# Attention and feed-forward on one core: float32 scores in two row halves, and a shorter rounding of the first batch's weights

## The chip, the cores and the metric

The kernel runs on one core of a Trainium2 chip. The metric is the time of one execution on the device in microseconds; the figure for a kernel is the median of several runs. The profile is of one execution. The engines are TensorE (PE, its weight loads PEld), VectorE (DVE), ScalarE (ACT), GpSimd (POOL) and SyncE (SP), which here only issues transfers.

## The reference

Causal attention for 4 batches of 12 heads (448 positions, 64 numbers a head), then a feed-forward layer with a layer norm ahead and a residual. Inputs are float32, but the two weight matrices reach the kernel as float64 words.

```python
scores = (1 / sqrt(64)) * matmul(q, k.T)          # per batch and head: 448 x 448
scores = where(triu(ones, k=1), -1e9, scores)
attn = exp(scores - max(scores))
attn = attn / (sum(attn) + 1e-09)
a = matmul(attn, v)                               # heads side by side: x is 448 x 768
xn = (x - mean(x)) / sqrt(var(x) + 1e-06) * g_ln
out = x + maximum(xn @ w_ch1, 0) @ w_ch2          # 768 -> 3072 -> 768
```

## The kernel before, in words

Heads go in pairs (6 pairs a batch), and a head's 448 rows in four blocks of 112. Row block `i` needs only the first 112 x (i + 1) columns of the scores, so a head has 112 + 224 + 336 + 448 = 1120 columns.

**Feed-forward.** Every product is made of three float32r products of high and low parts: `wh` with `xh`, `wh` with `xl`, `wl` with `xh` (L416), and likewise for the second layer (L435). `ffn` is a generator that yields after every 18 products of 448 columns; such a piece is a *slot*. A batch has 48 slots. The accumulators `ph` and `po` have two buffers. After a `ph`, ScalarE writes `hh` (Relu, L421) and VectorE `hl` (L422).

**Weights.** 48 units of 128 x 768 words, one per slot. In the first batch a unit is loaded as float64 words (`raw`, five buffers), rounded to float32, kept in DRAM for the later batches (`keep`), and split into `wh` (ScalarE, L116) and `wl` (L121). Rounding is `convert1` (GpSimd L93 and ScalarE L96, both from the high words) and `convert2` (two passes of VectorE, L101 and L105). `wl` is made by GpSimd in the first batch, by VectorE in the others. `weights_ahead` puts these steps into the slots: a unit used in slot s is begun in slot s - 4, with `convert2`, `split1` and `split2` one, two and three slots later. The first four units are rounded while batch 0's attention runs.

**Attention.** `scores` gives TensorE the products of a group of row blocks; VectorE reduces each block with the mask and finds its minimum (L237), `exps` is ScalarE's, `norm` multiplies by the reciprocal of the sum (GpSimd in batch 0, VectorE later; L267), `transposes` turns the probabilities (L283) and `pv` multiplies by v (`px`, L298), float32, with the two heads in the two column halves of the array. Scores of batch 0 are one float32 product over all 128 rows (L222), with the other head's rows of q filled with zeros by GpSimd (L166, L167). Scores of the later batches are two float32r products (L229): `split1` and `split2` make `qs` (q rounded in the upper 64 rows, its remainder in the lower) and `kh`, `kl`, on ScalarE (L187), VectorE (L188, L195) and GpSimd (L198).

**What sets the order.** All engines' queues are in the order in which the code is written. The lists at the top say in which slot, counted from the pair's own, each group of scores (`SAT`), of transposes (`TAT`), each head's norm (`NAT`) and the pair's `pv` (`END`) stand; the names with a 0 are batch 0's, which has no slots of products around it. In a slot the loop writes the steps of `pre` (loads, exponentials, norm), then the weights' steps, then 18 products, then the steps of `post` (`pv`, transposes, scores). The attention of batch b + 1 is woven into batch b's feed-forward slots.

Of the kernel before, what the change touches and what calls it, by code (L numbers as in the profile page):

```python
# [19 lines left out]
P = 128  # L20
C = 112
# [8 lines left out]
SGROUPS = [[(0, 3)], [(0, 0), (0, 2)], [(0, 1), (1, 1)], [(1, 3)], [(1, 0), (1, 2)]]  # L30
# [8 lines left out]
TH0, TH = [38, 40], [18, 30]  # L39
ELAG = [2, 5, 7]  # L40
NDVE = 7
STATS = [(0, 3), (3, 5), (5, 6)]
OFF = [C * (i * (i + 1) // 2) for i in range(NC + 1)]
# [3 lines left out]
def kernel(ctx, tc, qk, v, w1, w2, g, out):  # L47
# [26 lines left out]
    raw, zs, w32, wh, wl = {}, {}, {}, {}, {}  # L74
# [77 lines left out]
    class Att:  # L152
# [10 lines left out]
        def load(self, p):  # L163
            if self.b == 0:
                r = (first_qk if p < 4 else more_qk)[:, p % 4 * 3:p % 4 * 3 + 3, :]
                nc.gpsimd.memset(r[D:, 0, :], 0.0)  # L166
                nc.gpsimd.memset(r[:D, 1, :], 0.0)  # L167
                nc.sync.dma_start(out=r[:D, 0:3:2, :], in_=qk[0, p][:D, 0:3:2, :])
                nc.sync.dma_start(out=r[D:, 1:3, :], in_=qk[0, p][D:, 1:4:2, :])
            else:  # L170
                r = sb.tile([P, 4, S], F32, tag="qkraw", name="qkraw", bufs=1)
                nc.sync.dma_start(out=r, in_=qk[self.b, p])
            if self.b == 0:
                vt = rest[:C, 2 * NC * D * p:2 * NC * D * (p + 1)]
# [4 lines left out]
            self.t["raw", p], self.t["v", p] = r, vt  # L179

        def split1(self, p):
            r = self.t["raw", p]
            qs = sb.tile([P, 2, S], F32R, tag="qs", name="qs", bufs=1)
            kh = sb.tile([P, 2, S], F32R, tag="kh", name="kh", bufs=1)
            kl = sb.tile([P, 2, S], F32R, tag="kl", name="kl", bufs=1)
            rq, rk = r[:, 0:2, :], r[:, 2:4, :]
            nc.scalar.activation(out=qs, in_=rq, func=ACTF.Copy)  # L187
            nc.vector.tensor_copy(kh, rk)  # L188
            self.t["qk", p] = qs, kh, kl

        def split2(self, p):
            r = self.t.pop(("raw", p))
            qs, kh, kl = self.t["qk", p]
            rq, rk = r[:, 0:2, :], r[:, 2:4, :]
            nc.vector.tensor_tensor(  # L195
                out=qs[D:], in0=rq[D:], in1=qs[D:].bitcast(F32), op=ALU.subtract
            )
            nc.gpsimd.tensor_tensor(out=kl, in0=rk, in1=kh.bitcast(F32), op=ALU.subtract)  # L198

        def scores(self, p, grp):  # L200
            if self.b == 0:
                tag, bufs = (("sc", 3), ("sc", 3), ("sc", 3), ("mm", 2), ("mm", 2))[self.turn % 5]
                self.turn += 1
            else:
                tag, bufs = "sc", 3
# [155 lines left out]
        def steps(self):  # L361
# [4 lines left out]
            def put(where, t, f, *a):  # L366
                where.setdefault(t, []).append((f, a))
# [168 lines left out]
```

## Time and profile before

| | before |
|---|---|
| median of 3 runs | 960.81 us (958.25 to 961.01) |
| span of the profiled execution | 955.6 us |
| median less that span | 5.2 us |
| TensorE, busy | 908.6 us, 95% |
| VectorE, busy | 626.7 us, 66% |
| ScalarE, busy | 416.8 us, 44% |
| GpSimd, busy | 283.1 us, 30% |
| chain that ended last, TensorE's share | 65% |
| memory traffic over the span | 150 GB/s |

The span runs from the first to the last instruction of the one profiled execution; that execution has no time of its own beside it, so the median of the runs stands for it. Busy shares are means over stages that differ, so they don't say what bounds a stage. TensorE's products are pipelined: a product's duration in a row is longer than the distance from its start to that of the next.

### The profile page before, as it was taken

The page shows a single profiled execution, that of the slowest core. Times are in us where ns is not written, and L with a number is a line of the kernel's source. Part 1 is how long each engine was busy: PE and PEld are TensorE (multiplying, and loading weights), DVE is VectorE, ACT ScalarE, POOL GpSimd, SP SyncE. Part 2 cuts the span into 40 slices and gives each one's busy share as a digit, 9 for nine tenths or more (in the row PEclk, how much of TensorE's full clock was granted, in tenths as well). Part 3 has the DMA queues.
Part 4 walks back from the last instruction along what each step waited for, and adds up shares of the span by engine and source line. Part 5 has one row for each costly group of instructions (what it writes and reads, how often), then busy time and mean ns, then how long its engine had stood idle before and what let it go on. Part 6 is the DMA issues. An engine that isn't in the chain of part 4 may idle for free.

```text
span 955.6 us, 13000 instructions
## 1 busy us (share of the span) xinstructions
PE 908.6 (95%) x4864; PEld 794.1 (83%) x4864; DVE 626.7 (66%) x1208; ACT 416.8 (44%) x859; POOL 283.1 (30%) x211
## 2 busy tenths in 40 slices
PE   6888988998998799999999999999999999999998
PEld 4556877887787698898888998898888999999997
DVE  5978999999989746656565566666665544333432
ACT  6754565547553344444543245443443233323320
POOL 7654675887758901111010311110010210000000
PEclk9988998999999999999999999999999999999999
DMA  9730667767677654332322463323322243233310
GB/s 252 270 112 1 213 232 270 250 221 278 217 249 239 234 192 147 115 135 80 134 80 76 150 226 115 139 87 137 115 100 76 98 165 116 100 103 119 108 56 36
DMA packets 35246, 144.36 MB, mean 151 GB/s; under 512 B 4080, under 2 KB 8688, under 8 KB 35184
## 3 DMA queue, kind: packets, MB, share of 16 engines
q1 hardware_dynamic: 35184, 143.54, 43.5%
q8 instruction: 38, 0.62, 0.3%
q14 instruction: 24, 0.20, 0.1%
HBM read 119.15 MB, written 24.38 MB: 150 GB/s over the span
## 4 chain that ended last, share of the span: by engine, by line
PE 65%; POOL 0%; DVE 0%; ACT 0%; issue 0%; POOLq 0%; ACTq 0%
PE po L435 29%; PE ph L416 28%; PE sc L229 3%; PE px L298 3%; PE pt L283 2%; PE pln L311 1%; POOL wl L121 0%; PE rb L336 0%; PE mb L331 0%; DVE w L105 0%; ACT wh L116 0%; DVE xT L439 0%; POOL xl L356 0%; POOLq L121 0%; ACTq L116 0%
## 5 line engine op out<-in xcount | busy, mean ns | idle before, releaser
L435 PE MATMUL po<-hh,wl 128*128 128x448 f32 x576 | 212.7, 369 | 8.7 <-POOL wl L121 8.7
L416 PE MATMUL ph<-xh,wh 128*128 128x448 f32 x576 | 215.2, 374 | 3.4 <-DVE hl L422 2.0
L435 PE MATMUL po<-hh,wh 128*128 128x448 f32 x576 | 215.6, 374 | 0.0
L416 PE MATMUL ph<-xl,wh 128*128 128x448 f32 x576 | 212.1, 368 | 0.5 <-POOL xl L356 0.5
L416 PE MATMUL ph<-xh,wl 128*128 128x448 f32 x576 | 211.4, 367 | 1.0 <-POOL wl L121 1.0
L435 PE MATMUL po<-hl,wh 128*128 128x448 f32 x576 | 212.0, 368 | 0.0
L422 DVE SCALAR_TENSOR_TENSOR hl<-ph,hh 128x448 fp32r<-128x448 f32 x96 | 59.7, 622 | 128.1 <-ACT hh L421 128.1
L116 ACT ACTIVATE wh<-full 128x768 fp32r<-128x768 f32 x144 | 119.5, 839 | 54.8 <-PE po L435 50.8
L121 DVE TENSOR_TENSOR wl<-full,wh 128x768 fp32r<-128x768 f32 x144 | 136.3, 953 | 0.8 <-ACT wh L116 0.5
L198 POOL TENSOR_TENSOR kl<-qkraw,kh 128x896 fp32r<-128x896 f32 x18 | 48.2, 2678 | 278.8 <-DVE kh L188 267.3
L251 ACT ACTIVATE P<-P,nm 112x448 f32<-112x448 f32 (+3 forms) x176 | 91.7, 522 | 81.9 <-DVE nm L237 77.9
L435 PEld LDWEIGHTS po<-hh,wl 128*128 128x128 f32 x576 | 109.2, 190 | 20.4 <-POOL wl L121 11.6
L421 ACT ACTIVATE hh<-ph 128x448 fp32r<-128x448 f32 x96 | 51.9, 540 | 162.8 <-PE ph L416 162.7
L416 PEld LDWEIGHTS ph<-xh,wh 128*128 128x128 f32 x576 | 109.2, 190 | 13.0 <-DVE hl L422 2.3
L416 PEld LDWEIGHTS ph<-xh,wl 128*128 128x128 f32 x576 | 108.9, 189 | 10.3 <-POOL wl L121 1.7
L435 PEld LDWEIGHTS po<-hh,wh 128*128 128x128 f32 x576 | 109.4, 190 | 8.5
L416 PEld LDWEIGHTS ph<-xl,wh 128*128 128x128 f32 x576 | 109.1, 189 | 8.8 <-POOL xl L356 0.9
L435 PEld LDWEIGHTS po<-hl,wh 128*128 128x128 f32 x576 | 109.3, 190 | 8.2
L121 POOL TENSOR_TENSOR wl<-w,wh 128x768 fp32r<-128x768 f32 x48 | 103.2, 2151 | 36.8 <-issue 15.2
L439 DVE TENSOR_TENSOR xT<-po,xT 128x448 f32<-128x448 f32 x48 | 29.9, 622 | 115.6 <-PE po L435 115.6
L237 DVE CUSTOM_DVE_ANT_0 P<-sc,mask 112x448 f32<-112x448 f32 (+3 forms) x176 | 70.2, 443 | 38.2 <-PE sc L229 26.6
L105 DVE SCALAR_TENSOR_TENSOR w<-w,z 128x768 uint32<-128x768 uint32 x48 | 90.0, 1875 | 3.1
(64 smaller groups left out, 1049.0 us busy)
## 6 DMA issues: line engine op xcount, KB each, us to landing
full<-scratch SPq DMA_DIRECT2D x72, 768.0 KB, 4.2
raw<-w_dram SPq DMA_DIRECT2D x48, 768.0 KB, 4.9
scratch<-w SPq DMA_DIRECT2D x48, 384.0 KB, 2.7
qkraw<-qk_dram SPq DMA_DIRECT2D x18, 896.0 KB, 7.2
out_dram<-xT SPq DMA_DIRECT2D x24, 224.0 KB, 2.0
vt<-v_dram SPq DMA_DIRECT2D x18, 224.0 KB, 5.6
first_qk<-qk_dram SPq DMA_DIRECT2D x8, 224.0 KB, 5.3
rest<-v_dram SPq DMA_DIRECT2D x6, 224.0 KB, 7.4
```

The costliest lines, as they stand in the source:

```text
L105: nc.vector.scalar_tensor_tensor(out=w, in0=w, scalar=3, in1=z, op0=ALU.logical_shift_left, op1=ALU.bitwise_or)
L116: nc.scalar.activation(out=wh[s], in_=w32[s], func=ACTF.Copy)
L121: eng.tensor_tensor(out=wl[s], in0=w32[s], in1=wh[s].bitcast(F32), op=ALU.subtract)
L198: nc.gpsimd.tensor_tensor(out=kl, in0=rk, in1=kh.bitcast(F32), op=ALU.subtract)
L229: nc.tensor.matmul(pt[:, o:o + n], lhsT=qs[:, h, C * i:C * i + C], rhs=kk[:, h, :n], start=(part == 0), stop=(part == 1),)
L237: nc.vector.tensor_tensor_reduce(out=self.t["P", p, h][:, OFF[i]:OFF[i + 1]], in0=pt[:, o:o + n], in1=mask[:, S - n:], op0=ALU.add, op1=AL ...
L251: nc.scalar.activation(out=pp, in_=pp, func=ACTF.Exp, scale=-1.0, bias=nm[:, x:x + 1], accum_out=self.t["sm", p, h][:, i:i + 1],)
L416: nc.tensor.matmul(pm[y], lhsT=w[:, c * P:c * P + P], rhs=z[:, c, :], start=(c == 0 and i == 0), stop=(c == KC - 1 and i == 2),)
L421: nc.scalar.activation(out=hh[:, x + y, :], in_=pm[y], func=ACTF.Relu)
L422: nc.vector.scalar_tensor_tensor(out=hl[:, x + y, :], in0=pm[y], scalar=0.0, in1=hh[:, x + y, :].bitcast(F32), op0=ALU.max, op1=ALU.subtract,)
L435: nc.tensor.matmul(pm, lhsT=w[:, o:o + P], rhs=z[:, x, :], start=(x == 0 and i == 0), stop=(x == HF - 1 and i == 2),)
L439: nc.vector.tensor_tensor(out=a.xT[:, m, :], in0=pm, in1=a.xT[:, m, :], op=ALU.add)
```

## The change

Rounding: `convert1` is two passes of ScalarE, a Prelu with two slopes on the high words and a copy from integers, with a scale, on the low words. `convert2` is one pass of VectorE. GpSimd has no part in it, and `wl` is always VectorE's. Scores: q and k are loaded once per head, one head into the upper 64 rows and one into the lower, and each row block of each head is one float32 product over 64 rows, for all batches. Nothing is split or filled with zeros. A group is now a list of row blocks for both heads, each head with an accumulator of its own, and three slots hold a pair's scores. Norm, transposes and `pv` of a later pair stand one slot later, and the probabilities have four buffers instead of three.

```diff
-SGROUPS = [[(0, 3)], [(0, 0), (0, 2)], [(0, 1), (1, 1)], [(1, 3)], [(1, 0), (1, 2)]]
+SGROUPS = [[3], [0, 2], [1]]
...
-SAT0, TAT0, NAT0, END0, EV0 = [-1, 0, 2, 2, 4], [7, 8, 9, 10, 11], [4, 6], 13, [1, 1, 0, 1, 0]
-SAT, TAT, NAT, END, EV = [0, 0, 1, 1, 2], [3, 4, 4, 5, 5], [3, 4], 6, [1, 1, 0, 0, 0]
+SAT0, TAT0, NAT0, END0, EV0 = [-1, 1, 3], [7, 8, 9, 10, 11], [5, 6], 13, [1, 1, 0, 1, 0]
+SAT, TAT, NAT, END, EV = [0, 1, 2], [4, 5, 5, 6, 6], [4, 5], 7, [1, 1, 0, 0, 0]
...
     def convert1(s):
-        high = raw[s][:, :, 1].bitcast(F32)
-        zs[s] = sb.tile([P, UH], F32, tag="z", name="z", bufs=3)
+        bits[s] = sb.tile([P, UH], U32, tag="bits", name="bits", bufs=3)
         w32[s] = sb.tile([P, UH], F32, tag="w32", name="w32", bufs=4)
-        nc.gpsimd.tensor_scalar(
-            out=zs[s], in0=high, scalar1=0.0, scalar2=1.0, op0=ALU.mult, op1=ALU.mult
+        nc.scalar.activation(
+            out=w32[s], in_=raw[s][:, :, 1].bitcast(F32), func=ACTF.Prelu, scale=2.0 ** -112,
+            alpha=2.0 ** 32,
         )
-        nc.scalar.activation(out=w32[s], in_=high, func=ACTF.Copy, scale=2.0 ** -112)
+        nc.scalar.activation(
+            out=bits[s], in_=raw.pop(s)[:, :, 0], func=ACTF.Copy, scale=LAST * 2.0 ** -29
+        )
 
     def convert2(s):
         ready.add(s)
-        z, w = zs.pop(s).bitcast(U32), w32[s].bitcast(U32)
+        w = w32[s].bitcast(U32)
         nc.vector.scalar_tensor_tensor(
-            out=z, in0=raw.pop(s)[:, :, 0], scalar=29, in1=z,
-            op0=ALU.logical_shift_right, op1=ALU.bitwise_or,
-        )
-        nc.vector.scalar_tensor_tensor(
-            out=w, in0=w, scalar=3, in1=z, op0=ALU.logical_shift_left, op1=ALU.bitwise_or
+            out=w, in0=w, scalar=3, in1=bits.pop(s), op0=ALU.logical_shift_left,
+            op1=ALU.bitwise_or,
         )
...
     def split2(s):
         wl[s] = sb.tile([P, UH], F32R, tag="wl", name="wl", bufs=4)
-        eng = nc.gpsimd if s < ns else nc.vector
-        eng.tensor_tensor(
+        nc.vector.tensor_tensor(
             out=wl[s], in0=w32[s], in1=wh[s].bitcast(F32), op=ALU.subtract
         )
...
-                r = (first_qk if p < 4 else more_qk)[:, p % 4 * 3:p % 4 * 3 + 3, :]
-                nc.gpsimd.memset(r[D:, 0, :], 0.0)
-                nc.gpsimd.memset(r[:D, 1, :], 0.0)
-                nc.sync.dma_start(out=r[:D, 0:3:2, :], in_=qk[0, p][:D, 0:3:2, :])
-                nc.sync.dma_start(out=r[D:, 1:3, :], in_=qk[0, p][D:, 1:4:2, :])
-            else:
-                r = sb.tile([P, 4, S], F32, tag="qkraw", name="qkraw", bufs=1)
-                nc.sync.dma_start(out=r, in_=qk[self.b, p])
-            if self.b == 0:
+                r = first_qk[:, 2 * p:2 * p + 2, :]
                 vt = rest[:C, 2 * NC * D * p:2 * NC * D * (p + 1)]
                 vt = vt.rearrange("p (h j d) -> p h j d", h=2, j=NC)
             else:
+                r = sb.tile([P, 2, S], F32, tag="qkraw", name="qkraw", bufs=2)
                 vt = sb.tile([C, 2, NC, D], F32, tag="v", name="vt", bufs=2)
+            nc.sync.dma_start(out=r[:D], in_=qk[self.b, p][:D, 0:3:2, :])
+            nc.sync.dma_start(out=r[D:], in_=qk[self.b, p][D:, 1:4:2, :])
             nc.sync.dma_start(out=vt, in_=v[self.b, p])
...
-                if self.b == 0:
-                    r = self.t["raw", p]
+            r = self.t["qk", p]
+            o = 0
+            for i in grp:
+                n = C * (i + 1)
+                for h in range(2):
                     nc.tensor.matmul(
-                        pt[:, o:o + n], lhsT=r[:, h, C * i:C * i + C], rhs=r[:, 2, :n],
-                        start=True, stop=True,
+                        tiles[h][:, o:o + n], lhsT=r[D * h:D * h + D, 0, C * i:C * i + C],
+                        rhs=r[D * h:D * h + D, 1, :n], start=True, stop=True,
                     )
-                else:
-                    qs, kh, kl = self.t["qk", p]
-                    for kk, part in ((kh, 0), (kl, 1)):
-                        nc.tensor.matmul(
-                            pt[:, o:o + n], lhsT=qs[:, h, C * i:C * i + C], rhs=kk[:, h, :n],
-                            start=(part == 0), stop=(part == 1),
-                        )
                 o += n
...
                 if self.b:
                     put(pre, t0 - 4, self.load, p)
-                    put(pre, t0 - 2, self.split1, p)
-                    put(pre, t0 - 1, self.split2, p)
```

Where the instructions then stand. TensorE first, at a later pair's `pv` in the full stretches. `sc` are the scores, `px` the product with v, and each row is a product with its result's rows and columns. Before:

```order
L298 MATMUL px<-PT,vt 64x448 x2
L298 MATMUL px<-PT,vt 64x336 x2
L298 MATMUL px<-PT,vt 64x224 x2
L298 MATMUL px<-PT,vt 64x112 x2
L229 MATMUL sc<-kh,qs 112x448
L229 MATMUL sc<-kl,qs 112x448
L229 MATMUL sc<-kh,qs 112x112
L229 MATMUL sc<-kl,qs 112x112
L229 MATMUL sc<-kh,qs 112x336
L229 MATMUL sc<-kl,qs 112x336
```

And of the change, at the same place:

```order
L278 MATMUL px<-PT,vt 64x448 x2
L278 MATMUL px<-PT,vt 64x336 x2
L278 MATMUL px<-PT,vt 64x224 x2
L278 MATMUL px<-PT,vt 64x112 x2
L206 MATMUL sc<-qkraw 112x112 x2
L206 MATMUL sc<-qkraw 112x336 x2
```

Behind `px` stood one head's blocks 3, 0 and 2; now blocks 0 and 2 of both heads stand there, block 3 of both a slot before and block 1 of both a slot later.

VectorE, in batch 0's attention, where the second early unit is rounded (`z` and `w` are L101 and L105; `r` is the reciprocal that releases GpSimd's norm; `ISA P,nm<-sc` is the reduction of a score block). Before:

```order
L262 TENSOR_SCALAR r<-sm 112x4
L263 RECIPROCAL r<-r 112x4
L237 ISA rest,nm<-sc,mask 112x112
L237 ISA nm 112x1
L237 ISA rest,nm<-sc,mask 112x336
L237 ISA nm 112x1
L101 SCALAR_TENSOR_TENSOR z<-raw,z 128x768
L105 SCALAR_TENSOR_TENSOR w_283<-w_283,z 128x768
L237 ISA rest,nm<-sc,mask 112x224
```

And of the change:

```order
L242 TENSOR_SCALAR r<-sm 112x4
L243 RECIPROCAL r<-r 112x4
L126 TENSOR_TENSOR wl<-w_182,wh 128x768
L110 SCALAR_TENSOR_TENSOR w_274<-w_274,bits 128x768
L216 ISA rest,nm<-sc,mask 112x112
L216 ISA nm 112x1
L216 ISA rest,nm<-sc,mask 112x336
```

The two passes of one unit have become the `wl` of the unit before and one pass, and the reductions that stood between the reciprocal and the first pass now stand behind both.

ScalarE, in one slot of the first layers with exponentials in it (`hh` is the Relu). Before:

```order
L251 ACTIVATE P,sm<-P,nm 112x448
L251 ACTIVATE P,sm<-P,nm 112x112
L251 ACTIVATE P,sm<-P,nm 112x336
L96 ACTIVATE w_1186<-raw 128x768
L116 ACTIVATE wh<-w_1074 128x768
L421 ACTIVATE hh<-ph 128x448
```

And of the change:

```order
L231 ACTIVATE P,sm<-P,nm 112x112
L231 ACTIVATE P,sm<-P,nm 112x336
L231 ACTIVATE P,sm<-P,nm 112x112
L231 ACTIVATE P,sm<-P,nm 112x336
L99 ACTIVATE w_1207<-raw 128x768
L103 ACTIVATE bits<-raw 128x768
L122 ACTIVATE wh<-w_1080 128x768
L399 ACTIVATE hh<-ph 128x448
```

One more pass of 128 x 768 stands ahead of the Relu, and the exponentials of a slot are those of both heads.

## Rows read from the trace of the kernel before

**Rows 1.** Busy time by stage: stretch, its length, each engine, granted clock, DMA share, GB/s.
```profile
0.00:84.00 84.00, 66.29 (x368) 42.09 (x368) 62.24 (x178) 48.82 (x143) 45.29 (x79) 0.93 0.58 180
84.00:100.00 16.00, 13.21 (x54) 11.31 (x55) 15.60 (x28) 9.56 (x18) 9.90 (x10) 0.85 0.17 53
100.00:340.00 240.00, 217.14 (x1150) 187.77 (x1150) 218.60 (x300) 125.50 (x235) 180.17 (x98) 0.97 0.69 239
340.00:558.00 218.00, 218.00 (x1216) 195.25 (x1215) 133.63 (x311) 92.75 (x198) 25.29 (x13) 1.00 0.36 125
558.00:776.00 218.00, 218.00 (x1216) 195.26 (x1215) 132.82 (x310) 91.93 (x197) 22.48 (x12) 1.00 0.34 120
```

**Rows 2.** TensorE's waits, 84 to 340 us: total us, times, longest.
```profile
PE pt L283 <- DVE P L267: 13.1, 11, 2.5
PE po L435 <- POOL wl L121: 8.7, 7, 1.9
PE ph L416 <- DVE hl L422: 2.0, 1, 2.0
PE ph L416 <- ACT xh L353: 1.4, 1, 1.4
PE ph L416 <- POOL wl L121: 1.0, 2, 0.5
```

**Rows 3.** Chain of waits, one pair of batch 2: start, us, what.
```profile
565.44 0.92 PE sc L229 x6
...
570.02 0.81 PE sc L229 x6
...
574.49 0.51 PE sc L229 x4
...
591.60 2.04 PE px L298 x16
593.64 1.10 PE sc L229 x6
```

**Rows 4.** Timeline of TensorE in batch 0, scores and then px: start, us.
```profile
20.40 1.68 PE L222 MATMUL sc<-first_qk 128*112 128x448 f32 x6
22.01 2.11 PE L298 MATMUL px<-PT,rest 112*64 112x448 f32 x16
```

**Rows 5.** Groups of VectorE, 84 to 340 us: busy us, mean ns; idle before.
```profile
L105 DVE SCALAR_TENSOR_TENSOR w<-w,z 128x768 uint32<-128x768 uint32 x44 | 86.1, 1957 | 2.7
L101 DVE SCALAR_TENSOR_TENSOR z<-raw,z 128x768 uint32<-128x768 uint32 x44 | 54.1, 1230 | 0.2
...
L195 DVE TENSOR_TENSOR qs<-qkraw,qs 64x896 fp32r<-64x896 f32 x5 | 11.5, 2292 | 0.2
...
L121 DVE TENSOR_TENSOR wl<-full,wh 128x768 fp32r<-128x768 f32 x1 | 0.9, 950 | 0.0
```

**Rows 6.** Groups of ScalarE, 84 to 340 us.
```profile
L96 ACT ACTIVATE w<-raw 128x768 f32<-128x768 f32 x44 | 39.6, 900 | 0.0
L116 ACT ACTIVATE wh<-w 128x768 fp32r<-128x768 f32 x44 | 37.0, 840 | 32.2 <-DVE w L105 32.1
...
L187 ACT ACTIVATE qs<-qkraw 128x896 fp32r<-128x896 f32 x6 | 5.7, 955 | 3.4 <-DMA qkraw<-qk_dram 3.4
```

**Rows 7.** Line L105: shortest, median and longest duration in ns.
```profile
L105 DVE SCALAR_TENSOR_TENSOR w<-w,z x48: 957/1625/6049, 16.5 to 325.7; 128x768 uint32<-128x768 uint32 x48
```

**Rows 8.** Timeline of VectorE in batch 0's attention.
```profile
8.07 0.62 DVE L237 CUSTOM_DVE_ANT_0 P<-sc,mask 112x448 f32<-112x448 f32 x1 [8.07 <-POOL mask L476]
...
23.01 4.45 DVE L101 SCALAR_TENSOR_TENSOR z<-raw,z 128x768 uint32<-128x768 uint32 x1
...
53.68 4.12 DVE L195 TENSOR_TENSOR qs<-qkraw,qs 64x896 fp32r<-64x896 f32 x1
```

**Rows 9.** Timeline of GpSimd there: one head's norm, then a unit's wl.
```profile
22.93 1.95 POOL L267 TENSOR_SCALAR rest<-rest,r 112x112 f32<-112x112 f32 x4
24.80 1.84 POOL L121 TENSOR_TENSOR wl<-w,wh 128x768 fp32r<-128x768 f32 x1
```

More of the change, by code (lines that the diff above doesn't have):

```diff
@@ L42 @@
 STATS = [(0, 3), (3, 5), (5, 6)]
+LAST = 239 / 256
 OFF = [C * (i * (i + 1) // 2) for i in range(NC + 1)]
@@ L73 @@
     ready = set()
-    raw, zs, w32, wh, wl = {}, {}, {}, {}, {}
+    raw, bits, w32, wh, wl = {}, {}, {}, {}, {}
     def load_raw(s):
@@ L191, in split2 @@
-        def split2(self, p):
-            r = self.t.pop(("raw", p))
-            qs, kh, kl = self.t["qk", p]
-            rq, rk = r[:, 0:2, :], r[:, 2:4, :]
-            nc.vector.tensor_tensor(
-                out=qs[D:], in0=rq[D:], in1=qs[D:].bitcast(F32), op=ALU.subtract
-            )
-            nc.gpsimd.tensor_tensor(out=kl, in0=rk, in1=kh.bitcast(F32), op=ALU.subtract)
-        def scores(self, p, grp):
-            if self.b == 0:
-                tag, bufs = (("sc", 3), ("sc", 3), ("sc", 3), ("mm", 2), ("mm", 2))[self.turn % 5]
-                self.turn += 1
-            else:
-                tag, bufs = "sc", 3
-            pt = ps.tile([C, S], F32, tag=tag, name="sc", bufs=bufs)
-            nm = sb.tile([C, 2], F32, tag="nm", name="nm", bufs=8)
-            o = 0
-            for h, i in grp:
-                n = C * (i + 1)
+            self.t["qk", p], self.t["v", p] = r, vt
@@ L211, in scores @@
+        def scores(self, p, grp):
+            tiles = []
+            for h in range(2):
+                if self.b == 0:
+                    tag, bufs = (("sc", 3), ("sc", 3), ("sc", 3), ("mm", 2), ("mm", 2))[self.turn % 5]
+                    self.turn += 1
+                else:
+                    tag, bufs = "sc", 3
+                tiles.append(ps.tile([C, S], F32, tag=tag, name="sc", bufs=bufs))
                 if ("P", p, h) not in self.t:
                     x = 2 * p + h
-                    if self.b == 0 and x % 5 >= 3:
-                        a = 2 * NC * D * NP + (x % 5 - 3) * OFF[NC]
-                        old = (x - 5) // 2, (x - 5) % 2
-                        assert x < 5 or all(("T", *old, j) in self.done for j in range(NC))
+                    if self.b == 0 and x % 6 >= 4:
+                        a = 2 * NC * D * NP + (x % 6 - 4) * OFF[NC]
+                        old = (x - 6) // 2, (x - 6) % 2
+                        assert x < 6 or all(("T", *old, j) in self.done for j in range(NC))
@@ L217, in scores @@
                         self.t["P", p, h] = rest[:C, a:a + OFF[NC]]
                     else:
-                        self.t["P", p, h] = sb.tile([C, OFF[NC]], F32, tag="P", name="P", bufs=3)
-                if self.b == 0:
-                    r = self.t["raw", p]
+                        self.t["P", p, h] = sb.tile([C, OFF[NC]], F32, tag="P", name="P", bufs=4)
+            r = self.t["qk", p]
+            o = 0
+            for i in grp:
+                n = C * (i + 1)
+                for h in range(2):
@@ L233, in scores @@
-                o += n
-            o = 0
-            for x, (h, i) in enumerate(grp):
-                n = C * (i + 1)
-                nc.vector.tensor_tensor_reduce(
-                    out=self.t["P", p, h][:, OFF[i]:OFF[i + 1]], in0=pt[:, o:o + n],
-                    in1=mask[:, S - n:], op0=ALU.add, op1=ALU.min, scale=-0.125, scalar=3.0e38,
-                    accum_out=nm[:, x:x + 1],
-                )
-                o += n
-            self.t["nm", p, tuple(grp)] = nm
+                        tiles[h][:, o:o + n], lhsT=r[D * h:D * h + D, 0, C * i:C * i + C],
@@ new lines, in scores @@
+                        rhs=r[D * h:D * h + D, 1, :n], start=True, stop=True,
+                    )
+                o += n
+            for h in range(2):
+                nm = sb.tile([C, 2], F32, tag="nm", name="nm", bufs=8)
+                o = 0
+                for x, i in enumerate(grp):
+                    n = C * (i + 1)
+                    nc.vector.tensor_tensor_reduce(
+                        out=self.t["P", p, h][:, OFF[i]:OFF[i + 1]], in0=tiles[h][:, o:o + n],
+                        in1=mask[:, S - n:], op0=ALU.add, op1=ALU.min, scale=-0.125, scalar=3.0e38,
+                        accum_out=nm[:, x:x + 1],
+                    )
+                    o += n
+                self.t["nm", p, h, grp[0]] = nm
@@ L245, in exps @@
         def exps(self, p, grp):
-            nm = self.t.pop(("nm", p, tuple(grp)))
-            for x, (h, i) in enumerate(grp):
+            for h in range(2):
+                nm = self.t.pop(("nm", p, h, grp[0]))
                 if ("sm", p, h) not in self.t:
                     self.t["sm", p, h] = sb.tile([C, NC], F32, tag="sm", name="sm", bufs=6)
-                pp = self.t["P", p, h][:, OFF[i]:OFF[i + 1]]
-                nc.scalar.activation(
-                    out=pp, in_=pp, func=ACTF.Exp, scale=-1.0, bias=nm[:, x:x + 1],
-                    accum_out=self.t["sm", p, h][:, i:i + 1],
-                )
-                self.done.add(("exp", p, h, i))
+                for x, i in enumerate(grp):
+                    pp = self.t["P", p, h][:, OFF[i]:OFF[i + 1]]
+                    nc.scalar.activation(
+                        out=pp, in_=pp, func=ACTF.Exp, scale=-1.0, bias=nm[:, x:x + 1],
+                        accum_out=self.t["sm", p, h][:, i:i + 1],
+                    )
+                    self.done.add(("exp", p, h, i))
```

15 lines of the change are left out of this document (1 added, 14 removed).

## The prediction

> **What bounds the kernel now.** I read the busy times by stage first, then TensorE's waits in the stage that is not full, then the chain of waits, and only then the groups of instructions that the change touches.
>
> The stages [rows 1]: 0 to 84 us is the attention of batch 0; from 84 us TensorE multiplies the feed-forward layers, one batch to a stretch, with the attention of the next batch woven in. From 340 to 776 us TensorE is busy in every microsecond, and the last stretch holds products alone. There an edit counts only by what it adds to or takes from TensorE. The stretch 84 to 340 us does about the same products as each of the two behind it, yet takes 256 us instead of 218. VectorE is busy for 234 of those 256 us (15.60 and 218.60), GpSimd for 190.
>
> What TensorE waited for there [rows 2]: 13.1 us for VectorE's normalised probabilities, 8.7 + 1.0 us for GpSimd's `wl`, 3.4 us for other things when the layers begin, together 26.2. The granted clock was 0.85 in the first 16 us and 0.97 in the next 240, so 2.4 + 7.2 us of full-speed work were lost to stretches at 1.2 GHz. 26.2 + 9.6 is 36 of the 38 us.
>
> Why VectorE is full there: its two passes on a raw weight, L105 and L101, take 86.1 and 54.1 us [rows 5]. L105 ranges from 957 ns to 6049 with a median of 1625 [rows 7]. It is one shape throughout; what differs is whether GpSimd runs beside it. The L101 at 23.01 us shows how: it takes 4.45 us [rows 8], and in that time lie GpSimd's norm of a head, 1.95 us, and its `wl`, 1.84 [rows 9]; 0.7 us are left. The Trainium skill, "SBUF — State Buffer", on the ports, says that VectorE (with two SBUF inputs) and GpSimd hold a shared pair of ports exclusively, and that the loser blocks for the whole instruction; the 4.45 us row agrees with it for these two.
>
> **The change, part by part.** (a) *Rounding, batch 0's weights (48 units).* GpSimd loses its pass and the `wl` subtraction, VectorE loses L101, ScalarE gains a pass. In 84 to 340 us VectorE sheds 54.1 (L101), takes L105 at its free duration, 44 x 0.957 = 42.1 instead of 86.1, and gains 44 `wl` at 0.95 (the one L121 row) = 41.9. L195, 11.5 us there, goes with the old scores. VectorE: 234 - 54 - 44 + 42 - 11.5 = 166 us. ScalarE: 135 + 44 x 0.900 for the new pass - 5.7 for L187 = 169 us [rows 1, 5, 6]. Neither Prelu nor the pass from integers stands in the trace. The bounds are the two weight passes of the same size, 840 ns (plain input) and 900 (every second word) [rows 6]; I take 900 because the input is strided in the same way. Only one table load is in the changed program as well, so no switch is added. So in about 230 us both engines have a quarter free.
>
> Then `wl` no longer arrives late, and the normalisation is no longer behind a 2 us L105 in VectorE's queue: 22.8 of the 26.2 us go. The start (3.4 us) stays, since its causes (the first `xh`, the first `hl`) are untouched. The 7.2 us of half clock behind the waits go with them; the 2.4 of the start stay. Against it: a slot's ScalarE work grows to 0.90 + 0.90 + 0.84 = 2.64 us of weights, ahead of the Relu on which VectorE's `hl`, and then TensorE, wait, in a slot of 218 / 48 = 4.5 us. In slots with exponentials the Relu will be late now and then: I add 3 us, as many as the start costs now, with 0 and 15 (half of the gain) as ends. **Gain here 30 - 3 = 27 us**, before the scores.
>
> (b) *Scores, batches 1 to 3.* VectorE, ScalarE and GpSimd each lose work (L195, L188, L187, L198), but from 340 us on they are idle for much of the time, so that is worth nothing there. TensorE: per pair of heads, before, three stretches of 0.92 + 0.81 + 0.51 us, and 1.10 instead of 0.92 when `px` stands ahead: 2.42 [rows 3]. After: one float32 product for each head and row block. Full-height float32 is in the trace for batch 0: 896 columns in 1.61 us (20.40 to 22.01), 1.8 ns a column, 4 clocks at 2.4 GHz being 1.67 [rows 4]. A pair has 2 x 1120 columns: 3.73 us if the two heads' products run one behind the other, 1.87 if the row halves run at once. No row shows row halves. The nearest is `px`, float32 too, whose two heads are written to the two column halves: 2 x 1120 columns in 2.04 us [rows 3], 0.91 ns each, half of the above. So column halves do run at once, and I take row halves to do the same.
>
> But `px` also shows what a change of shape costs: 2.04 - 1.87 = 0.17 us on the way in, and 1.10 - 0.92 = 0.18 on the way out. Plain 128-row work in float32r, as now, costs nothing between it and the layers' products. In the new order the scores stand at three places per pair, one of them right behind `px`. The Trainium skill, "TensorEngine Tiling (Array Packing)", section Tiling Modes, says that a change of the tiling mode drains TensorE; the trace agrees with 0.17 and 0.18 us for column halves. By row the sum is 1.87 + 3 x 0.35 = 2.92, and I add 0.05 for the smallest blocks, as long as their weight loads: 2.97, which is **0.55 us more per pair**. Without a cost of switching it would be 1.87 + 0.18 = 2.05, 0.37 less per pair; with heads in turn 3.73 + 1.05 = 4.8, 2.4 more. Twelve pairs lie in the two full stretches: **+6.6 us** (-4.4 to +29); five of batch 1's in the stretch before: **+2.8 us** (-1.9 to +12).
>
> (c) *Batch 0's attention, 0 to 84 us.* The four early weight units are rounded here, three of them with an L101 like the one of 4.45 us [rows 8], held up by GpSimd's norm and `wl` [rows 9]. GpSimd's `wl` goes. The norm stays, and the new order puts VectorE's `wl` and then the one shift directly behind the reciprocal that releases it. So VectorE still blocks: I take 1.95 us per unit, one head's norm; 0 and 3.8, both heads', are the ends. Per unit: now 4.45 + 0.96 = 5.4, after 1.95 + 0.95 + 0.96 = 3.9. That is 1.5 less, for three units 4.5; the first unit gains nothing. The L195 of 4.12 us at 53.68 [rows 8], behind which pair 5's reductions and a copy queue, is gone. The first reduction waits until 8.07 us [rows 8] for GpSimd's mask, behind twelve fillings with zeros that go; it will wait for the first scores instead, for which I allow 1 us. Scores at half the TensorE time help little where VectorE sets the pace. Of the sum, 4.5 + 4 + 1 = 9.5, I count three quarters, **7 us**, as ScalarE's queue per early pair grows by 0.9 and takes the pace from VectorE. Ends: 0 and 14.
>
> (d) *DMA.* A later pair loads half the bytes of q and k, in two issues on SP instead of one; no wait on a load of q and k is among TensorE's [rows 2] after the first microseconds. Nothing.
>
> Sum: -7 - 27 + 2.8 + 6.6 = -24.6 on a span of 955.6, so 931.0. The median of the runs, 960.81, lies 5.2 above that span; the same 5.2 gives **936 us**.
>
> **Rivals.**
> *Row halves in turn (slower).* If the two heads' products do not overlap, the change does not do what its layout says. Then 17 pairs cost 2.4 us more: +41. With -27 and, TensorE having no relief, -4 in batch 0, the time is 971. It decides from 1.8 us per pair on, where 17 pairs eat the 31. For it: no row shows row halves. Against it: `px`. Chance 0.14.
> *ScalarE becomes the bound of the first layers.* A slot of Relu, exponentials, copies and three weight passes then ends after TensorE's, and half of the 30 us stay as waits for `hl`: 936 + 12 = 948; with batch 0 as long as now, 955. For it: 2.64 us in each slot, in order, ahead of the Relu. Against it: 169 busy of 230. Chance 0.16.
> *The larger gain.* Row halves switch without a cost and batch 0 shrinks by its 14: -14 - 30 - 1.9 - 4.4 is -50, so 911; with one of the two, about 920. Chance 0.15.
> *As summed,* 926 to 946: chance 0.55.
>
> The range leaves out the first rival and the far end of the larger gain: 917 to 956. A measurement of this kernel can tell about 0.3%, 2.9 us, from no change. Faster by more: 0.55 + 0.16 + 0.15, less 0.02 for sums of both bad ends, 0.84; slower 0.12; within 0.3%, 0.04.
>
> **What the profile after should show.** Scores of the two heads overlapping in time, and a chain in which a pair's scores take 2.97 us in all (2.05 if switching is free); the two full stretches at 221 us each. The shift pass near 0.96 us in the layers, but with a `wl` of nearly 3 us ahead of it in batch 0. GpSimd near idle from 100 us. The first layers' stretch near 232 us, its waits for `wl` and normalised probabilities gone, those for `hl` a little up. Batch 0 ending near 77 us. Wrong would be: heads in turn (every stretch grows); a ScalarE over nine tenths in the first layers with TensorE waiting for `hl`; or a batch 0 as long as now, since the block has only moved to `wl`.

## The result, and the profile after

The changed kernel takes 932.69 us (median of 4 runs, 932.61 to 933.03), the kernel before 959.53 (957.74 to 961.01): a ratio of 0.9725, interval 0.9709 to 0.9741. Forecast were 936 us, within 917 to 956. The medians fell by 26.8 us. The profiled span fell from 955.6 to 931.2 us, by 24.4; the sum of the terms was 24.6. That is closer than the terms themselves came: their errors, as the table shows, happen to cancel. Stages are compared in one profiled execution of each kernel. The kernel before took 957.3 to 964.9 us over all the comparisons below, and its profiled execution is among the shortest. Full stretches of the same code agree within 0.1 us from kernel to kernel, so what scatters is batch 0 and the first layers, and differences of 2 or 3 us there are rough.

Stages are counted below from a batch's first `ph` product to the next batch's, in the profiled executions.

| stage, us | before | after | moved by | forecast |
|---|---|---|---|---|
| batch 0's attention | 84.2 | 78.7 | -5.5 | -7 |
| first layers | 255.4 | 227.1 | -28.3 | -24.2 |
| full stretches, both | 436.8 | 446.2 | +9.4 | +6.6 |
| last layers | 179.3 | 179.2 | -0.1 | 0 |
| sum | 955.6 | 931.2 | -24.4 | -24.6 |

The stages of the changed kernel, in the same columns as [rows 1]:

```profile
0.00:78.70 78.70, 62.20 (x368) 36.68 (x368) 47.46 (x177) 51.41 (x146) 30.11 (x58) 0.92 0.62 181
78.70:94.70 16.00, 13.81 (x60) 11.99 (x61) 9.89 (x19) 10.70 (x20) 6.95 (x6) 0.88 0.28 93
94.70:305.80 211.10, 209.77 (x1142) 176.49 (x1142) 145.13 (x295) 152.54 (x271) 9.69 (x7) 1.00 0.76 258
305.80:528.90 223.10, 222.57 (x1217) 188.58 (x1216) 122.70 (x299) 87.72 (x192) 8.81 (x7) 1.00 0.34 110
```

In the first layers behind their start TensorE is now busy for 209.8 of 211.1 us, at a granted clock of 1.00. Over the whole stage of 227 us VectorE has fallen to 155 us, ScalarE has risen to 163, and GpSimd works for 17. TensorE's waits in the stage, where [rows 2] had 26.2 us, are 4.6, of which these are the longest:

```profile
PE ph L394 <- DVE hl L400: 1.7, 1, 1.7
PE ph L394 <- ACT xh L333: 1.4, 1, 1.4
PE po L413 <- DVE wl L126: 0.5, 1, 0.5
```

The weight passes there, first VectorE's and then ScalarE's groups (compare [rows 5, 6]):

```profile
L110 DVE SCALAR_TENSOR_TENSOR w<-w,bits 128x768 uint32<-128x768 uint32 x44 | 47.7, 1085 | 2.2 <-ACT bits L103 2.2
L126 DVE TENSOR_TENSOR wl<-w,wh 128x768 fp32r<-128x768 f32 x44 | 41.8, 951 | 0.0
```

```profile
L99 ACT ACTIVATE w<-raw 128x768 f32<-128x768 f32 x44 | 39.7, 902 | 0.2 <-DVE wl L126 0.2
L103 ACT ACTIVATE bits<-raw 128x768 uint32<-128x768 uint32 x44 | 39.2, 892 | 0.0
L122 ACT ACTIVATE wh<-w 128x768 fp32r<-128x768 f32 x44 | 36.8, 837 | 1.4 <-DVE w L110 1.4
```

The pass that stayed, L105 before and L110 now, fell from 1957 to 1085 ns in the same shape.

The price of the scores is read from the chain of waits. One pair of batch 2 in the changed kernel, from one `px` to the next:

```profile
564.34 2.04 PE px L278 x16
566.38 0.95 PE sc L206 x8
567.33 3.83 PE ph L394 x18
571.16 0.57 PE sc L206 x4
571.73 7.48 PE ph L394 x36
...
579.59 3.66 PE ph L394 x18
...
588.52 0.94 PE sc L206 x4
589.46 3.86 PE po L413 x18
```

A place where score products stand between other products is called a visit below; a pair has three. The `sc` rows are 0.95 + 0.57 + 0.94 = 2.46 us, hardly more than the 2.42 of [rows 3]. But the 18 products behind a visit take 3.83 and 3.86 us, where 18 undisturbed products take 3.66, and the 36 behind the one of 0.57 us take 7.48 instead of 7.32. The chain cuts at the start of the next instruction, so what a change of shape costs on the way out stands in the neighbour's row: with the 0.53 us of the three neighbours the pair's scores cost 2.99 us, for which the forecast had 2.97. The pair takes 28.98 us; with the old scores it is 28.32 to 28.40.

### The profile page after: what moved, and what is told of

The parts are those of the page before. It is cut to its first block, busy times and chain, and to the rows that moved or that the text cites. A ratio compares the mean times of both kernels' runs of the same rounds, so it can differ in the third digit from the quotient of the medians.

```text
span 931.2 us, 12729 instructions
## 1 busy us (share of the span) xinstructions
PE 906.6 (97%) x4864; PEld 764.3 (82%) x4864; DVE 511.7 (55%) x1172; ACT 438.3 (47%) x889; POOL 64.4 (7%) x85
## 4 chain that ended last, share of the span: by engine, by line
PE 89%; ACT 4%; DVE 4%; DMA 1%; issue 1%; SPq 1%; POOL 0%; ACTq 0%; DVEq 0%
PE po L413 36%; PE ph L394 35%; PE sc L206 6%; PE px L278 5%; PE pt L263 4%; ACT P L231 1%; PE pln L291 1%; DMA raw<-w_dram 1%; DVE xg L329 1%; DVE w L110 1%; ACT PT L266 1%; ACT w L99 1%; DVE xg L326 1%; PE rb L316 0%; DVE wl L126 0%
## 5 line engine op out<-in xcount | busy, mean ns | idle before, releaser
L413 PE MATMUL po<-hh,wl 128*128 128x448 f32 x576 | 211.1, 367 | 0.6 <-DVE wl L126 0.5
L263 PE MATMUL pt<-ident,P 112*112 112x112 f32 x440 | 56.9, 266 | 7.3 <-ACT PT L266 4.0
L263 PEld LDWEIGHTS pt<-ident,P 112*112 112x112 f32 x440 | 47.4, 136 | 19.4 <-ACT PT L266 6.1
L266 ACT COPY PT<-pt 112x448 f32<-112x448 f32 x72 | 36.7, 530 | 45.0 <-PE pt L263 44.9
```

The source lines that it names most:

```text
L263: nc.tensor.transpose(pt[:, o:o + C], pp[:, a:a + C], ident[:C, :C])
L266: nc.scalar.copy(out=t[:, :o], in_=pt[:, :o])
L413: nc.tensor.matmul(pm, lhsT=w[:, o:o + P], rhs=z[:, x, :], start=(x == 0 and i == 0), stop=(x == HF - 1 and i == 2),)
```

## The experiments

**Each half of the change alone.** The first kernel has the old scores and the new rounding (`convert1`, `convert2` and `split2` as changed, all else as before); the second has the new scores with the old rounding, GpSimd's `wl` included.

```diff
 # rounding alone: the kernel before, with
+        nc.scalar.activation(out=w32[s], in_=raw[s][:, :, 1].bitcast(F32), func=ACTF.Prelu, ...)
+        nc.scalar.activation(out=bits[s], in_=raw.pop(s)[:, :, 0], func=ACTF.Copy, ...)
...
-        eng = nc.gpsimd if s < ns else nc.vector
-        eng.tensor_tensor(
+        nc.vector.tensor_tensor(
```

> The new rounding with the old scores. My theory (the first layers were held by VectorE's two passes on each raw weight, stretched by GpSimd's work beside them): the first layers' stretch falls from 255 us to 224 to 230, the two full stretches stay at 218.4 each, batch 0 ends near 81 us; span about 923, time about 926, ratio to the kernel before 0.964. Rival (the relief came from the scores' splitting that went, L195 and GpSimd's kl): the first layers' stretch stays at 245 us or more, time 945 or more.

> The new scores with the old rounding (GpSimd's pass, two VectorE passes, wl on GpSimd). My theory: VectorE sheds only some 15 us of 234 in the first layers, so their stretch stays near 250 us; full stretches 223.1 each as with the whole change; batch 0 ends near 80 us; span about 956, time about 959, the same as the kernel before within 0.7%. Rival (the splitting was what held the first layers): their stretch falls below 235 us, time below 945.

Rounding alone: 918.82 us, ratio 0.9568 (0.9544 to 0.9591). Scores alone: 964.72 us, ratio 1.005 (1.0026 to 1.0075).

| stage, us | before | rounding alone | scores alone | both |
|---|---|---|---|---|
| batch 0 | 84.2 | 76.5 | 87.1 | 78.7 |
| first layers | 255.4 | 223.4 | 252.8 | 227.1 |
| a full stretch | 218.4 | 218.4 | 223.2 | 223.1 |

The whole gain is the rounding's, and it is 42 us. Of the expectations, the theory held for the layers in both runs (the first layers with the rounding alone even fell just below the 224 expected); both missed batch 0, which ended 4.5 us earlier than expected with the rounding alone and 7 later with the scores alone. The scores cost 2.3 to 2.8 us in batch 0 and 4.7 in each full stretch. In the first layers their price depends on what bounds the stage: while TensorE waits for VectorE, losing L195 and its kin is worth 2.6 us; once TensorE is full, the scores cost 3.6. So the two effects don't add: the scores cost 3.8 us by the medians on the kernel before, and 13.9 behind the new rounding. The 2.6 and the 2.8 are rough, since the profiled execution of the scores alone is the longest of its five (967.15 us, median 964.72). The kernel that has only the rounding is 14 us faster than the change as made.

**The old scores back in batches 2 and 3 only.**

```diff
+            if self.b >= 2:
+                sat, tat, nat, end, ev = SAT2, TAT2, NAT2, END2, EV
+                groups, scores, exps, load = SGROUPS2, self.scores2, self.exps2, self.load2
```

> The change for batches 0 and 1, the old float32r scores with their splitting for batches 2 and 3. My theory (in the full stretches only TensorE counts, and it pays 4.7 us a stretch for the visits to the row halves): batch 0 and the first layers as with the change (78.7 and 227 us), full stretches back at 218.4 each; span about 922, time about 923.5, ratio to the kernel before 0.963. Rival (the 4.7 us a stretch come from the later slots of norm and pv or from elsewhere than the scores): stretches stay above 221 us, time 928 or more.

923.58 us (923.5 to 924.42), ratio 0.962 (0.9595 to 0.9645). Both full stretches are back at 218.4 us and the other stages where they were. The edit puts the earlier slots of norm, transposes and `pv` back as well, so by itself it doesn't separate the scores from their slots; the rows behind the visits, here and in the run with a fourth visit, do. The pair's chain here, for the comparison with the one above:

```profile
559.77 1.08 PE sc L222 x6
560.86 3.63 PE ph L468 x18
564.49 0.82 PE sc L222 x6
565.31 3.64 PE ph L468 x18
```

Behind these visits 18 products take 3.63 to 3.64 us: float32r over the full height leaves nothing in its neighbour.

**Both heads in the same row half, batches 2 and 3.**

```diff
+                nc.sync.dma_start(out=r[:D, 0:2], in_=qk[self.b, p][:D, 0:3:2, :])
+                nc.sync.dma_start(out=r[:D, 2:4], in_=qk[self.b, p][D:, 1:4:2, :])
...
+                    y, z = (D * h, 0) if self.b < 2 else (0, 2 * h)
...
-                        tiles[h][:, o:o + n], lhsT=r[D * h:D * h + D, 0, C * i:C * i + C],
+                        tiles[h][:, o:o + n], lhsT=r[y:y + D, z, C * i:C * i + C],
```

> The changed kernel, but in batches 2 and 3 both heads of a pair are loaded into the upper 64 rows, so that their products cannot share the array. The columns, the number of visits and the bytes are unchanged. It measures the first rival of the prediction. Theory A, the row halves run at once in the changed kernel and this takes it away: 1120 columns more for TensorE in each pair, 1.87 us, so each full stretch goes from 223.1 to about 234.3. Theory B, the overlap seen in the trace is only that of starts, and the two heads share the array's time: the stretches stay within 2 us of 223.1.

This kernel and the one with a fourth visit were executed once each. Here q and k have one buffer instead of two and are loaded a slot later; TensorE's waits in the full stretches are the 1.1 us of the changed kernel, so that cost it nothing. The profiled span is 952.9 us, each full stretch 234.4 us, 11.25 more than in the changed kernel or 1.87 a pair: Theory A to the hundredth. Its visits in the chain:

```profile
579.39 1.70 PE sc L211 x8
581.09 3.84 PE ph L399 x18
584.93 0.94 PE sc L211 x4
```

1.70 instead of 0.95 and 0.94 instead of 0.57, and the 3.84 behind them is the same. The third visit takes 1.68 instead of 0.94. So the row halves do run at once in the changed kernel, and the price is not in the columns.

**A fourth visit, batches 2 and 3.**

```diff
+SGROUPS4 = [[3], [2], [0], [1]]
+SAT4, TAT4, NAT4, END4, TH4 = [0, 1, 2, 3], [5, 6, 6, 7, 7], [5, 6], 8, [21, 33]
```

> The changed kernel, but in batches 2 and 3 a pair's scores stand in four slots instead of three (block 3, block 2, block 0, block 1), with the norm, transposes and product with v a slot later. Columns and arithmetic are unchanged. Theory A, the price of the new scores is a price per visit, paid at the way in and in the products behind it (0.2 + 0.17 us): one more visit a pair adds 0.37 us, so each full stretch goes from 223.1 to about 225.3 us. Theory B, the price is one of the columns or of the smallest blocks: the stretches stay at 223.1, within 0.5. The other stages do not change.

Span 934.4 us. An ordinary pair takes 29.31 to 29.41 us instead of 28.98 to 29.03, so 0.33 to 0.38 for one more visit. The stretches, however, are 224.8 and 223.8 us and the first layers 1.0 longer: 3.4 us over the 12 pairs, 0.28 each. The rest is given back where the first layer-norm transposes (`pln`) stand, 30.55 us instead of 30.67, and in the last period, 28.55 instead of 29.11. Theory A holds for the ordinary pair; over a stretch the price was smaller than expected. In the changed kernel this is the pair that holds a wait, here in its chain:

```profile
642.28 0.40 PE pt L263 x4
642.71 0.54 ACT PT L266
...
643.29 0.54 PE pln L291 x3
```

The chain leaves TensorE for 0.6 us while ScalarE empties the buffer that the next transposes want. The run with four visits had the `pln` groups a slot later and does not show this wait; a second one of 0.3 us, in the last period, it keeps.

**That slot alone.**

```diff
-TH0, TH = [38, 40], [20, 32]
+TH0, TH = [38, 40], [21, 33]
```

> The changed kernel with the two groups of layer-norm transposes of the later batches one slot later each. The trace of the changed kernel shows TensorE waiting 0.6 us once in each stretch, at a layer-norm transpose, for ScalarE to empty a buffer of the probabilities' transposes; the run with four visits, which had this shift in it, does not show that wait. Theory A: the wait is part of the price per stretch of the new order and can be moved away: each of the three stretches is 0.5 to 0.6 us shorter (222.5 instead of 223.1), the time 931. Theory B: the wait turns up at another transpose, and the stretches stay at 223.1.

935.07 us, ratio 0.9724 (0.9688 to 0.976), and neither theory: the full stretches grew to 223.95 us. The wait for ScalarE's copy stayed as it was, and in the next slot the next group of `pln` waits for a copy of VectorE's:

```profile
643.78 0.54 ACT PT L266
...
644.36 0.54 PE pln L291 x3
...
649.71 0.62 DVE PT L268
...
650.37 0.54 PE pln L291 x3
```

In the run with four visits the probabilities' transposes stood a slot later as well, which this run left where they were. TensorE's waits at `pln` came to 1.8 us in the two stretches, and to 1.1 in the changed kernel; the other 0.5 us a stretch that were lost are not accounted for.

**`wl` back on GpSimd, first batch.**

```diff
-        nc.vector.tensor_tensor(
+        eng = nc.gpsimd if s < ns else nc.vector
+        eng.tensor_tensor(
```

> The change, but the first batch's wl subtraction on GpSimd as before. Theory A (what counts is VectorE's sum of work): VectorE loses 42 us of wl and its shift pass grows from 1.08 to some 1.9 us beside GpSimd, the sum is about the same 155 of 227 us, TensorE hardly waits; time 932 to 937. Theory B (the shared ports themselves do the harm, by holding VectorE and making wl late): the first layers' stretch grows to 240 us or more, time 945 or more.

943.16 us, ratio 0.9818 (0.9791 to 0.9844); the first layers take 235.6 us instead of 227.1. The nearer expectation is B's, though its 240 and 945 were not reached and no `wl` is late. VectorE is busy for 129 us there, 26 less than in the changed kernel, and yet TensorE waits for it again. TensorE's costliest wait and two of VectorE's norm groups (390 and 331 ns in the changed kernel for these shapes):

```profile
PE pt L264 <- DVE P L248: 7.5, 8, 1.9
```

```profile
L248 DVE TENSOR_SCALAR P<-P,r 112x336 f32<-112x336 f32 x12 | 9.3, 773 | 0.0
L248 DVE TENSOR_SCALAR P<-P,r 112x224 f32<-112x224 f32 x12 | 7.3, 605 | 0.0
```

**A pass more on VectorE, first batch, none on GpSimd.**

```diff
+        nc.vector.scalar_tensor_tensor(
+            out=bits[s], in0=bits[s], scalar=0, in1=bits[s], op0=ALU.logical_shift_left,
+            op1=ALU.bitwise_or,
+        )
```

> The changed kernel with one more pass of VectorE over each of the 48 units of the first batch (the result of ScalarE's second pass is combined with itself, which leaves it as it is). GpSimd gets no work back. It tells apart what relieved the first layers: fewer passes of VectorE, or passes that no longer stand beside GpSimd's. Theory A, the blocking beside GpSimd was the price: 44 free passes of 0.95 us take VectorE from 155 to about 197 us of 227, TensorE waits a little more in slots with norms and reductions, and the stage grows from 227 to 229 to 232 us, the time to 935 to 938. Theory B, the number of VectorE's passes was the price: the waits for normalised probabilities come back, the stage takes 238 us or more, the time is 945 or more.

941.75 us, ratio 0.9796 (0.9756 to 0.9836). The first layers take 232.55 us, 5.5 more and just past the end of A's 229 to 232; batch 0, which the expectation had left out, takes 2.3 more. VectorE works for 196 of 232.6 us, 67 more than with `wl` on GpSimd, and the stage is 3 us shorter than there. The waits are of another kind, four late `wl`:

```profile
PE po L417 <- DVE wl L130: 4.8, 4, 1.5
```

So a pass too many costs something, but this GpSimd pass beside VectorE costs more than a VectorE pass.

**Batch 0, three attempts to shorten it, and one on the faster kernel.** First, two of ScalarE's three copies of transposed probabilities to VectorE, on the changed kernel and on the one with the rounding alone (the edit is the same):

```diff
-EV0 = [1, 1, 0, 1, 0]
+EV0 = [0, 1, 0, 0, 0]
```

> The changed kernel, but in batch 0 two of the three copies of transposed probabilities that ScalarE makes for each pair go to VectorE, which is less busy there (26 of 34 us against 30). Theory A, ScalarE's load sets the pace of batch 0 after the change: a pair's period falls by up to 1.1 us from 8.55, and batch 0 goes from 78.7 to about 74 us, the time to 928. Theory B, the order of the steps within a pair (scores, reduction, exponential, norm, transposes, one behind the other) sets it: batch 0 stays within 1 us of 78.7, the time at 932 to 933. Theory C, VectorE becomes the next bound and batch 0 grows, to 80 us or more.

> The old scores with the new rounding, the fastest version so far (918.8 us, batch 0 in 76.5 us), with the same two copies of each of batch 0's pairs moved from ScalarE to VectorE. Theory A, ScalarE's load sets batch 0's pace there (29 of 34 us busy, and most of the chain): batch 0 falls by 3 to 5 us to about 72, the time to about 915. Theory B, VectorE at 28 of 34 us is as near its limit, and with the copies becomes the bound: batch 0 in 77 us or more, and the time 919 to 923.

935.14 us, ratio 0.9756 (0.9734 to 0.9779), batch 0 in 80.7 us, 2.0 later; and 918.7 us, ratio 0.9577 (0.9549 to 0.9604), batch 0 in 78.4, 1.9 later. (Four other runs with the changed kernel's batch 0 end it between 77.9 and 78.8 us, so the first is clear of that scatter.) On the changed kernel ScalarE's work from 24 to 58 us fell from 30.4 to 25.3 us, VectorE's rose from 26.0 to 28.7, and a pair took 8.8 to 9.0 us instead of 8.5 to 8.6 even before the granted clock fell to 1.2 GHz at 49 us. Less load on ScalarE does not shorten a pair there. On the other kernel it does: the first three pairs take 7.9 us instead of 8.2. What makes its batch 0 later lies behind them, where the granted clock was at 1.2 GHz from 48 to 55 us. From 24 to 58 us, without and with the copies moved (the clock is the third figure from the end):

```profile
24.00:58.00 34.00, 31.27 (x196) 20.09 (x194) 28.10 (x90) 29.01 (x86) 20.04 (x33) 1.00 0.71 260
24.00:58.00 34.00, 31.31 (x181) 21.00 (x181) 29.45 (x93) 25.45 (x73) 18.18 (x29) 0.90 0.71 262
```

Why the clock fell in the second and not in the first is not shown. Then the second head's norm to VectorE, on the same two kernels:

```diff
-            eng = nc.vector if self.b or p >= NDVE else nc.gpsimd
+            eng = nc.vector if self.b or h == 1 else nc.gpsimd
```

> The changed kernel, but in batch 0 VectorE normalises the second head of each pair and GpSimd only the first. With the new groups both heads' exponentials end together, and GpSimd has the two norms one behind the other. Theory A, this queue of norms sets a pair's period in batch 0: GpSimd's two norms of 1.9 to 3.3 us become one, the period falls from 8.55 by 1 us or more, batch 0 ends near 73 us instead of 78.7 and the time is about 927. Theory B, the chain through reductions, exponentials and transposes sets it, with VectorE's own queue in it: batch 0 ends between 77 and 80. Theory C, VectorE, at 26 of 34 us, gets too much: later than 80.

> The old scores with the new rounding (918.8 us, batch 0 in 76.5 us), and in batch 0 the norm of each pair's second head on VectorE. With the old groups the first head is ready some slots before the second, so GpSimd's two norms do not queue. Theory A, with nothing queued nothing is won, and VectorE, at 28 of 34 us, takes longer: batch 0 in 76.5 to 79 us, the time 919 to 921. Theory B, GpSimd's norms hold the pace here too: batch 0 in 74 us or less, the time 916 or less.

937.72 us, ratio 0.9761 (0.971 to 0.9811), batch 0 in 80.9 us, which is Theory C's; and 921.65 us, ratio 0.9589 (0.9551 to 0.9626), batch 0 in 80.0, 1 us past Theory A's range. (Of the first, two executions took 935 us and two 940; the profiled one is of the faster two.) The pairs take 9.2 us instead of 8.5 to 8.6, and 8.8 instead of 8.2 at a granted clock of 1.00. Taking a norm off GpSimd does not shorten a pair either: on VectorE it becomes part of the chain, with `wl` and the shift behind it. What holds a pair of the changed kernel is in its chain, here for one pair of batch 0:

```profile
35.31 1.00 PE sc L206 x8
36.31 0.26 DVE P L216
...
36.61 1.07 ACT P L231 x4
...
37.89 0.74 ACT P L231 x3
38.64 0.42 ACT PT L266
39.06 0.04 issue
39.10 0.98 PE pt L263 x8
```

Behind the scores of blocks 0 and 2 of both heads the chain leaves TensorE: ScalarE does the four exponentials (each with the read of its sum) and then a copy of transposed probabilities that is queued behind them. TensorE's waits from 24 to 58 us:

```profile
PE pt L263 <- ACT PT L266: 3.3, 4, 1.3
PE pt L263 <- POOL P L247: 0.9, 2, 0.5
PE pt L263 <- POOL rest L247: 0.6, 1, 0.6
```

With the rounding alone the scores take TensorE longer, and yet between 18 and 47 us it waits nowhere for more than 0.2 us. In the run with two copies moved, the chain still goes from the exponentials through a copy of ScalarE's, the one of three that the edit left there, and at other places through a moved copy that now stands behind VectorE's `wl` and shift. Moving only the copy that the chain names was not tried.

## Why the prediction was right, point by point

**(a) First layers: right, and a little too careful.** Forecast -27 without the scores. Rounding alone gives -31.9. The 3 us set aside for late Relus were not needed: the wait for `hl` is 1.7 us, the one of the layers' start. The durations chosen for what no row showed were good: 902 and 892 ns for the two ScalarE passes (900 taken), 951 for `wl` (950), and 0.95 for the shift pass except where it stands beside GpSimd's `xl` (mean 1085, 957 taken). VectorE came to 155 us where 166 were summed, although its shift pass took 47.7 and not 42.1: the sum counted only L105 as held up, but the norms (L267, 25.7 us before, 17.4 after) and the additions ahead of the reciprocals (5.6 and 1.9) had been held up too, and it left out L188's 3.7, which also went. Two experiments show what the blocking between VectorE and GpSimd is worth here: `wl` on GpSimd again costs 8.5 us although VectorE does less, a pass more on VectorE alone 5.5.

**(b) Scores: right in kind, too small.** Row halves run at once, and their price is the change of shape. Forecast +0.55 us a pair, +6.6 in the two stretches and +2.8 in the first layers; measured +0.55 to +0.71 for an ordinary pair, +9.4 and, behind the new rounding, +3.6. The step had priced three switches per pair, and a pair's own rows and neighbours came out as priced (2.99 us for 2.97). Per stretch 4.7 us were measured for 3.3. Of these, 2.7 lie in the five periods from `px` to `px` (146.7 us after, 144.0 with the old scores), among them the waits at `pln` transposes, 0.5 us of idle TensorE, which the step did not have. The other 2.0 lie outside: 1.8 ahead of the first `px`, where the first pair's three visits and now also the second pair's first stand, 3.40 us of rows where the old scores have 2.24, with the longer neighbours behind them.

**(c) Batch 0: nearly the right sum from wrong parts.** Forecast -7, measured -5.5. The forecast held that VectorE's `wl`, directly behind the reciprocal that releases GpSimd's norm, would block. It is the norm that does. VectorE and GpSimd there, in the changed kernel:

```profile
34.05 0.93 DVE L126 TENSOR_TENSOR wl<-w,wh 128x768 fp32r<-128x768 f32 x1
34.89 0.95 DVE L110 SCALAR_TENSOR_TENSOR w<-w,bits 128x768 uint32<-128x768 uint32 x1
```

```profile
31.60 1.92 POOL L247 TENSOR_SCALAR rest<-rest,r 112x112 f32<-112x112 f32 x4 [2.80 <-ACT rest L231]
34.23 3.32 POOL L247 TENSOR_SCALAR rest<-rest,r 112x112 f32<-112x112 f32 x4 [0.71 <-DVE r L243]
```

`wl` and the shift start first and take their free 0.93 and 0.95 us; the norm that starts into them takes 3.32 us instead of 1.92, nearly all of it in the first of its four instructions (1.76 us instead of 0.39). In [rows 8, 9] it was VectorE's L101 that paid, begun 0.08 us after the norm; now the norm begins 0.18 us after `wl`. The later starter waits in both. The Trainium skill, "SBUF — State Buffer", section Who interferes with whom, says the same: the order of issue decides who blocks. The trace agrees; the step had taken VectorE for the later one without asking which instruction of a tie begins first. So the relief of VectorE was larger than summed: -7.8 with the rounding alone, which still has its L195. How much of that is the clock is not separated: from 24 to 58 us 0.85 was granted before and 1.00 with the rounding alone. What failed beside it is the sentence that scores in half the TensorE time "help little": they cost 2.3 to 2.8 us. The chain above shows one place: the scores of both heads come in one visit, so their four exponentials stand together in ScalarE's queue ahead of a copy that TensorE needs, and a pair takes 8.5 to 8.6 us instead of 8.2. More is lost earlier. The first `px` begins at 23.81 us in the changed kernel and at 21.11 with the rounding alone, 2.7 us sooner. Ahead of it, in the changed kernel, ScalarE is done with the first pair's exponentials at 11.85 us and then waits 2.8 us until the first raw weight is loaded, with the second pair's exponentials queued behind its passes on that weight; TensorE waits 2.0 us for the norms and 1.3 for ScalarE's copies; and its granted clock is at half, 1.2 GHz, from about 14 to 25 us. The first 24 us, in the changed kernel and with the rounding alone:

```profile
0.00:24.00 24.00, 16.42 (x58) 8.63 (x60) 9.49 (x42) 14.72 (x41) 7.19 (x21) 0.80 0.95 254
0.00:24.00 24.00, 17.29 (x83) 10.98 (x84) 12.53 (x51) 15.87 (x44) 15.27 (x36) 1.00 0.96 262
```

The nine other kernels with the new scores in batch 0 have that half clock too, the three others with the old scores don't. By the fourth `px` the gap is 3.9 us (49.55 and 45.65); the rounding alone then gives some of it back, where TensorE waits 2.4 us behind its L195. How the price divides among wait, clock and queue was not separated.

**(d) DMA: right.** No wait on q and k in the layers.

**The span and the median.** 5.2 us were added to the span, as before the change; the profiled span after it lies only 1.5 us below the median. That is the distance between 936 and 932.7. In every execution on record the time is 1.7 to 2.2 us above its own span, so some 3 us of the 5.2 were scatter: the span was that of one of the shorter executions of the kernel before.

**The rivals.** Heads in turn would have cost (234.4 - 218.4) / 6 = 2.66 us a pair against before, where 2.4 was priced; but they don't go in turn. ScalarE stayed at 163 of 227 us in the first layers and TensorE's waits for it there are those of the start and of `pln`, 1.9 us. The larger gain was there in the rounding and was spent by the scores.

## What to carry over

Change one thing at a time where two edits share a diff: this one was a gain of 42 us and a loss of 14, and only the half kernels show it. Where a stage is full of TensorE, price an edit by what its neighbours' rows become, since the cost of switching a shape stands behind the switched products. In a stage made of queues, as batch 0 is, compare the granted clock of the stretch too before naming an engine as the one that sets the pace. And read a slow pass of VectorE beside GpSimd's timeline before counting passes: moving `wl` from GpSimd to VectorE shortened by 8.5 us a stage in which TensorE waited for VectorE.

## What was not expected of the hardware

- VectorE's norm is held up too, with one tile as input and one number a partition: 773 ns for 112 x 336 beside GpSimd's `wl` instead of 390. That is a mean: three of the twelve took 1.93 us, each begun 0.18 to 0.20 us behind a `wl`, the other nine 0.38 to 0.39. Two of the 112 x 224 began 0.01 us ahead of a `wl` by the record and waited as well.
- Two float32 products in row halves cost hardly more TensorE time than one (0.57 us for 224 columns of both heads, 0.94 in turn). Yet over the two full stretches they are dearer than twice as many float32r products over the full height, by 0.79 us a pair: 2.46 us of own rows against 2.42, with the switches and the waits at `pln` on top.
